# Linear attention with a gated projection: bonus products, one decay per unit, more load buffers, and another place for the output projection

## The chip, the cores and the metric

The kernel runs on one core of a Trainium2 chip. The metric is the device time of one execution in microseconds (us), the median of several executions. "Span" is the time from the first to the last instruction that the trace of an execution shows. The span is listed to 0.1 us.

The engines are TensorE (PE, with its weight loads as PEld), VectorE (DVE), ScalarE (ACT), GpSimd (POOL) and SyncE (SP, which issues the loads and stores).

## The reference

An attention of the RWKV kind: each head keeps a 48 x 48 state that decays by `w` at each step, and the newest token gets a bonus `u`. Its result goes into a gated linear unit whose gate is a causal convolution over five steps.

```python
# r, k, v: (4, 8, 768, 48); w, u: (8, 48); all float32
for t in range(S):
    cur = einsum('bhd,bhe->bhde', u * k[t], v[t])            # bonus of the newest token
    y[t] = einsum('bhd,bhde->bhe', r[t], state + cur)
    state = w * state + einsum('bhd,bhe->bhde', k[t], v[t])
x = y.transpose(0, 2, 1, 3).reshape(B, S, 384)
gate = sigmoid(causal depthwise conv of x, 5 taps)
out = (gate * (x @ w_val)) @ w_out
```

## The kernel before

A chunk is 128 steps, and two chunks are a unit. Each of the four sequences has three units, so there are twelve. The state passes from unit to unit within a sequence. The bonus of a token is its `v` scaled by one number per head, `dv`; TensorE adds it into the attention output as a product of `dv` with the identity.

The functions that the change touches:

```python
ld  = tile_pool(name="ld",  bufs=6)    # k and v as loaded
ldr = tile_pool(name="ldr", bufs=5)    # r as loaded

def state(n, cl):                      # KV: k^T v of one chunk
    kv_ps = ...                        # an own PSUM tile for each chunk
    for p in range(NP):
        matmul(out=kv_ps[:, p], lhsT=ks[:, cl, p], rhs=v of two heads, start=(p == 0), ...)

def carry(n, cl):                      # ID: adds the state that came in
    vector.tensor_tensor(out=kv_ps, in0=kv_ps, in1=zin, op=add)

def decay(n, cl):                      # ZE: state of the next chunk
    z = wk.tile(...)
    vector.tensor_tensor(out=z, in0=kv_ps, in1=wcm, op=mult)     # wcm = w**128

def y_out(n, cl):                      # Y: attention output, transposed
    # [cut: 12 narrow products of the state with r, 16 of scores with v]
    for G in range(3 * NP):            # the bonus: 12 products of 32 columns, last
        mm(G, dv[:, cl, 32 * G : 32 * G + 32], ident, last=True)

def project(n, cl):                    # O: three products 128 x 384
    o_ps = ps_at.tile(...)             # the PSUM pool (4 buffers) that the scores A use too
```

The order of work is written by hand. For units 4 to 11 it is this text, where `Y:-1.0` means chunk 0 of the unit before. Tokens of different engines run side by side; each engine takes its own in this order.

```
Y:-1.0 YE:-1.0 Y:-1.1 A:0.1 YE:-1.1 M:0.3 A:0.0 RS:1.0 M:0.2 KS:1.0 M:0.0 CV:0.0 C:-1.0
S:0.0 M:0.1 RT:1.0 V:-1.0 SE:0.0 SG:-1.0 HT:-1.0 V:-1.1 KV:0.0 SG:-1.1 RE:1.0 HT:-1.1
ID:0.0 KT:1.0 KE:1.0 O:-1.1 O:-1.0 OE:-1.1 ZE:0.0 PR:1.0 KV:0.1 ID:0.1 OE:-1.0 ZE:0.1
DV:0.0
```

Y attention output, A scores, C convolution, S bonus sums, RT and KT transposes, V value products, KV state products and O output projection run on TensorE. M (masks), SE (copy of the sums), HT (gated products), ID, ZE and PR run on VectorE. The copies YE, OE, RE and KE, the cast CV of v and the sigmoid SG run on ScalarE; RS, KS and DV on GpSimd.

Of the kernel before, what the change touches and what calls it, by code (L numbers as in the profile page):

```python
# [8 lines left out]
F32 = mybir.dt.float32  # L9
# [7 lines left out]
def kernel(  # L17
# [21 lines left out]
    U = 2  # L39
# [5 lines left out]
    persist = ctx.enter_context(tc.tile_pool(name="persist", bufs=1))  # L45
    ld = ctx.enter_context(tc.tile_pool(name="ld", bufs=6))
    ldr = ctx.enter_context(tc.tile_pool(name="ldr", bufs=5))
    wk = ctx.enter_context(tc.tile_pool(name="wk", bufs=2))
# [48 lines left out]
    for dst, src in ((wt, w), (ut, u)):  # L97
# [15 lines left out]
    nc.vector.tensor_copy(io_f, io_i32)  # L113
    sc_k = consts.tile([128, 1], F32)
    nc.vector.tensor_scalar(
        sc_k, io_f, scalar1=-1.0, scalar2=float(C - 1), op0=ALU.mult, op1=ALU.add
    )
    io_m = consts.tile([128, 2], mybir.dt.int32)
    nc.vector.tensor_single_scalar(io_m, io_j, C - 1, op=ALU.bitwise_and)
    sc_r = consts.tile([128, 2], F32)  # L120
    nc.vector.tensor_copy(sc_r, io_m)
    nc.vector.tensor_scalar_add(sc_r, sc_r, float(-C))
# [20 lines left out]
    nc.scalar.activation(out=lnw_bc, in_=w_bc, func=AF.Ln)  # L143
    dk = consts.tile([128, H, D], F32)
    dr = consts.tile([128, H, 2, D], F32)
    for j in range(2):
        nc.scalar.activation(
            out=dr[:, :, j, :], in_=lnw_bc, func=AF.Exp, scale=sc_r[:, j : j + 1]
        )
    nc.scalar.activation(out=dk, in_=lnw_bc, func=AF.Exp, scale=sc_k)  # L150

# [27 lines left out]
    wcm = consts.tile([128, NP, 2, D], F32)  # L179
    nc.gpsimd.memset(wcm, 0.0)  # L180


# [74 lines left out]
    def scale_k(n, eng, cls=(0, U)):  # L257
        cs = slice(*cls)
        eng.tensor_tensor(  # L259
            out=ks_t[n % 3][:, cs, :, :, 0:D].rearrange("p c n a d -> p c (n a) d"),  # L260
            in0=k_st[n][:, cs],
            in1=dk[:, None, :, :].to_broadcast([128, cls[1] - cls[0], H, D]),
            op=ALU.mult,
        )
# [42 lines left out]
    def bonus(n):  # L307
        if n == 0:
            kv_ps = ps_mm.tile([128, 512], F32, name="mm_ps")
        else:  # L310
            kv_ps = ps_kv.tile([128, 512], F32, name="kv_ps")
            st["kv_tile", n, 0] = kv_ps
        s_ps = kv_ps[:, DM : DM + U * H].rearrange("p (c h) -> p c h", c=U)
# [53 lines left out]
    def state(n, cl, idle=0):  # L367
        ks, vb = ks_t[n % 3], vb_t[n % 4]
        kv_ps = st.get(("kv_tile", n, cl))
        if kv_ps is None:  # L370
            kv_ps = ps_kv.tile([128, 512], F32, name="kv_ps")
        warm(kv_ps[:, 0:C], idle)
        kv_ps = kv_ps[:, 0:DM].rearrange("p (n a d) -> p n a d", n=NP, a=2)
        for p in range(NP):
            nc.tensor.matmul(  # L375
                out=kv_ps[:, p],
                lhsT=ks[:, cl, p].rearrange("p a x -> p (a x)"),
                rhs=heads(vb[:, cl], H)[:, 2 * p : 2 * p + 2, :],
                start=(p == 0),
                stop=(p == NP - 1),  # L380
                skip_group_check=True,
            )
        st["kv_ps", n, cl] = kv_ps
# [5 lines left out]
    def decay(n, cl):  # L389

        z = wk.tile([128, NP, 2, D], BF16, name="z", bufs=6)
        nc.vector.tensor_tensor(out=z, in0=st["kv_ps", n, cl], in1=wcm, op=ALU.mult)  # L392
        nn, cc = (n, 1) if cl == 0 else (n + 1, 0)
        st["zin", nn, cc] = z

    def y_out(n, cl, idle=0):
# [3 lines left out]
        warm(y_ps[:, 0], idle)  # L400
        first = set()

        def mm(G, lt, rh, last=False):
# [4 lines left out]
                rhs=rh,  # L408
                start=q not in first,
                stop=last,  # L410
                skip_group_check=True,
            )
            first.add(q)

# [6 lines left out]
        for x in range(2):  # L421
            for h in range(H):
# [4 lines left out]
                    vb[:, cl, 64 * h + c0 : 64 * h + c0 + 32],  # L427
                    at[:, par, p, :],
                )
        for G in range(3 * NP):  # L430
            mm(G, dv[:, cl, 32 * G : 32 * G + 32], ident, last=True)
        st["y_ps", n, cl] = y_ps
# [201 lines left out]
    def ok(n):  # L634
# [18 lines left out]
        S:3.0 SE:3.0 RT:4.0 M:3.1 A:3.1 KV:3.0 ZE:3.0 M:3.3 RE:4.0 C:2.0 KV:3.1 KS:4.0 V:2.1  # L653
        SG:2.1 V:2.0 M:3.2 HT:2.1 SG:2.0 ID:3.1 O:1.0 OE:1.0 KT:4.0 HT:2.0 O:1.1 PR:4.0 O:2.1
        KE:4.0 O:2.0 ZE:3.1 OE:2.1 DV:3.0 OE:2.0 OE:1.1
    """
    STEP = """
        Y:-1.0 YE:-1.0 Y:-1.1 A:0.1 YE:-1.1 M:0.3 A:0.0 RS:1.0 M:0.2 KS:1.0 M:0.0 CV:0.0 C:-1.0
        S:0.0 M:0.1 RT:1.0 V:-1.0 SE:0.0 SG:-1.0 HT:-1.0 V:-1.1 KV:0.0 SG:-1.1 RE:1.0 HT:-1.1
        ID:0.0 KT:1.0 KE:1.0 O:-1.1 O:-1.0 OE:-1.1 ZE:0.0 PR:1.0 KV:0.1 ID:0.1 OE:-1.0 ZE:0.1  # L660
        DV:0.0
    """
    TAIL = """
        Y:11.0 Y:11.1 YE:11.0 YE:11.1 CL:11.0 CL:11.1 VL:11.0 GL:11.0 VL:11.1 HL:11.0 GL:11.1
        HL:11.1 OL:11.0 XL:11.0 OL:11.1 XL:11.1
    """
    HEAD_STEPS = 4
    KBUFS, RBUFS = 6, 5
    loads = LOADS.split()
# [26 lines left out]
    nc.scalar.activation(out=wct, in_=wt, func=AF.Ln)  # L696
    nc.scalar.activation(out=wct, in_=wct, func=AF.Exp, scale=float(C))
    for par in range(2):
# [55 lines left out]
    def run(text, i):  # L754
        for tok in text.split():
# [5 lines left out]
            if name not in ("WV", "WP", "WO", "TL"):  # L761
                if not ok(n) or (name in ("KV", "ID", "ZE") and c == NU * U - 1):
                    continue
                if name == "ID" and c == 0:
                    continue
# [39 lines left out]
```

## Time and profile before

| | before |
|---|---|
| time, median of 3 | 107.12 us (106.53 to 108.38) |
| span of the profiled execution | 107.2 us |
| TensorE / VectorE busy | 93.5 / 76.9 us |
| first mask of unit 4, of unit 11 | 42.25 us, 93.30 us |

The first mask of a unit is the handiest mark in this trace. It starts when the scores of the unit are ready, and the distance from one to the next is the length of a unit. The seven distances were 7.37, 10.09, 6.40, 6.99, 6.67, 6.41 and 7.12 us. The second holds a stop of TensorE.

The lines that carry the argument are in the prediction.

### The profile page before, as it was taken

The numbers are of one execution on the slowest core, as the hardware profiler recorded it, in microseconds if no ns is written. First come the engines' busy times: TensorE is split into PE (matmuls) and PEld (weight loads), VectorE is DVE, ScalarE is ACT, GpSimd is POOL, SyncE is SP. The second block draws the span as 40 slices with busy tenths as digits, with TensorE's granted clock in tenths as the row PEclk, the third lists the DMA queues.
The fourth block names the chain that finished last, engine by engine and source line by source line (L and its number), as shares of the span: only waits on it lengthen the run. The fifth ranks groups of instructions, "written<-read, shape, count | busy, mean of one in ns | idle before, by whom it ended". The sixth has DMA issues, their size and how long they took to land.

```text
span 107.2 us, 5221 instructions
## 1 busy us (share of the span) xinstructions
PE 93.5 (87%) x2301; PEld 74.7 (70%) x2301; DVE 76.9 (72%) x153; ACT 73.2 (68%) x122; POOL 64.4 (60%) x64
## 2 busy tenths in 40 slices
PE   4996775999999999999299999999999989999770
PEld 4694664777887876868187878867889777876730
DVE  5395965484969793798428789899869798894050
ACT  4179625935997949896076889776898868845520
POOL 7957487566929976496089079495793965023000
PEclk9999999557999999999859999999999999999999
DMA  0999969989998969989696969798999992310404
GB/s 11 219 234 231 238 113 169 312 254 254 211 193 173 241 123 251 185 160 270 111 209 172 224 133 247 146 257 156 217 256 358 367 362 99 111 45 6 147 6 147
DMA packets 67491, 20.41 MB, mean 190 GB/s; under 512 B 63494, under 2 KB 67468, under 8 KB 67468
## 3 DMA queue, kind: packets, MB, share of 16 engines
q1 hardware_dynamic: 66492, 19.97, 81.3%
q8 instruction: 18, 0.29, 1.2%
q10 hardware_dynamic: 976, 0.10, 0.7%
q14 instruction: 5, 0.04, 0.1%
HBM read 15.35 MB, written 4.72 MB: 187 GB/s over the span
## 4 chain that ended last, share of the span: by engine, by line
PE 45%; SPq 15%; DVE 11%; issue 9%; DMA 9%; POOL 5%; ACT 3%; DVEq 0%; POOLq 0%
SPq L71 10%; DMA r_st<-in_r_dram 9%; PE mm_ps L405 9%; PE mm_ps L453 7%; PE at_ps L509 5%; PE at_ps L475 4%; PE at_ps L244 4%; PE at_ps L347 4%; POOL rs L230 3%; DVE at L360 3%; DVE hT L497 2%; PE at_ps L484 2%; PE kv_ps L375 2%; DVE z L392 2%; DVE kv_ps L387 2%
## 5 line engine op out<-in xcount | busy, mean ns | idle before, releaser
L360 DVE TENSOR_TENSOR at<-at_ps,mask 128x512 bf16<-128x512 f32 x48 | 30.4, 683 | 7.5 <-PE at_ps L347 7.4
L332 POOL TENSOR_TENSOR dv<-v_st,s_sb 128x768 bf16<-128x768 f32 x12 | 17.7, 1476 | 25.7 <-DVE s_sb L329 24.4
L259 POOL TENSOR_TENSOR ks<-k_st,dk 128x768 bf16<-128x768 f32 x11 | 20.4, 1858 | 2.6 <-DMA k_st<-in_k_dram 1.6
L230 POOL TENSOR_TENSOR rs<-r_st,dr 128x768 bf16<-128x768 f32 x10 | 18.2, 1820 | 2.4 <-DMA r_st<-in_r_dram 2.4
L252 ACT COPY rT<-at_ps 128x1024 bf16<-128x1024 bf16 (+1 forms) x13 | 15.8, 1229 | 4.0 <-PE at_ps L244 4.0
L453 PE MATMUL mm_ps<-xT,cwd 64*64 64x128 bf16 (+1 forms) x440 | 12.7, 255 | 3.3 <-issue 2.7
L466 ACT ACTIVATE gate<-mm_ps 128x384 bf16<-128x384 f32 x22 | 9.6, 487 | 8.5 <-PE mm_ps L453 8.5
L497 DVE TENSOR_TENSOR hT<-at_ps,gate 128x384 bf16<-128x384 f32 x22 | 11.7, 555 | 4.8 <-PE at_ps L484 4.7
L292 ACT COPY kT<-tr_ps 128x1024 bf16<-128x1024 bf16 x11 | 11.2, 1015 | 5.4 <-PE tr_ps L283 3.5
L453 PEld LDWEIGHTS <-cwd 64*64 64x64 bf16 x440 | 11.0, 111 | 4.8 <-issue 3.6
L437 ACT CAST xT<-mm_ps 128x384 bf16<-128x384 f32 x24 | 11.5, 485 | 3.9 <-PE mm_ps L405 3.3
L509 PE MATMUL at_ps<-wout,hT 128*128 128x384 bf16 x66 | 13.5, 327 | 0.2
L392 DVE TENSOR_TENSOR z<-kv_ps,wcm 128x384 bf16<-128x384 f32 x20 | 11.1, 555 | 0.9 <-PE kv_ps L375 0.5
L521 ACT COPY o_sb<-at_ps 128x384 f32<-128x384 f32 x22 | 9.7, 490 | 2.8 <-PE at_ps L509 2.8
L475 PE MATMUL at_ps<-xT,wval 128*128 128x256 bf16 x66 | 11.5, 286 | 0.0
L268 ACT CAST vb<-v_st 128x768 bf16<-128x768 f32 x12 | 10.1, 841 | 0.0
L347 PE MATMUL at_ps<-rT,kT 48*128 48x128 bf16 x192 | 8.8, 225 | 1.5 <-ACT kT L292 1.3
L405 PE MATMUL mm_ps<-at,vb 128*32 128x128 bf16 x384 | 9.8, 223 | 0.3 <-DVE at L360 0.3
L387 DVE TENSOR_TENSOR kv_ps<-kv_ps,z 128x384 f32<-128x384 f32 x16 | 8.9, 557 | 0.9 <-PE kv_ps L375 0.9
L300 DVE TENSOR_TENSOR pr<-tr_ps,rT 128x1024 bf16<-128x1024 bf16 x11 | 7.6, 688 | 1.7 <-ACT kT L292 1.2
L509 PEld LDWEIGHTS <-hT 128*128 128x128 bf16 x66 | 5.7, 98 | 4.5 <-DVE hT L497 2.2
L244 PE MATMUL at_ps<-ident,rs 128*128 128x128 bf16 x96 | 8.2, 234 | 0.1
(94 smaller groups left out, 151.2 us busy)
## 6 DMA issues: line engine op xcount, KB each, us to landing
r_st<-in_r_dram SPq DMA_DIRECT2D x12, 384.0 KB, 5.4
k_st<-in_k_dram SPq DMA_DIRECT2D x24, 192.0 KB, 4.8
v_st<-in_v_dram SPq DMA_DIRECT2D x24, 192.0 KB, 4.9
out_dram<-o_sb SPq DMA_DIRECT2D x11, 384.0 KB, 5.1
wv_st<-in_moe_w_val_dram SPq DMA_DIRECT2D x1, 576.0 KB, 5.5
wo_st<-in_moe_w_out_dram SPq DMA_DIRECT2D x1, 576.0 KB, 6.3
out_dram<-o_l SPq DMA_DIRECT2D x1, 192.0 KB, 1.9
out_dram<-o_l ACTq DMA_DIRECT2D x1, 96.0 KB
```

The lines of the kernel that those rows point to most:

```text
L230: eng.tensor_tensor(out=rs_t[n % 2][:, :, ps[0] : ps[1], :, 0:D].rearrange("p s n a d -> p (n a) s d"), in0=r_st[n][:, hs], in1=dr[:, hs], ...
L252: nc.scalar.copy(out=st["rT", n][:, ps[0] : ps[1], :].rearrange("x n (i s) -> x s n i", s=2), in_=st["r_tr", n, ps[0]],)
L259: eng.tensor_tensor(out=ks_t[n % 3][:, cs, :, :, 0:D].rearrange("p c n a d -> p c (n a) d"), in0=k_st[n][:, cs], in1=dk[:, None, :, :].to_ ...
L332: eng.tensor_tensor(out=dv_t[n % 2].rearrange("p c (h d) -> p (c h) d", d=D), in0=v_st[n].rearrange("p c h d -> p (c h) d"), in1=st["s", n ...
L347: nc.tensor.matmul(out=at_ps[par][:, p, :], lhsT=kT[rows, p, cs], rhs=rT[rows, p, cs], start=(p == 0), stop=(p == NP - 1), skip_group_chec ...
L360: nc.vector.tensor_tensor(out=st["at", n, cl][:, par], in0=st["at_ps", n, cl][par], in1=mask[:, None, :].to_broadcast([128, NP, 128]), op= ...
L392: nc.vector.tensor_tensor(out=z, in0=st["kv_ps", n, cl], in1=wcm, op=ALU.mult)
L405: nc.tensor.matmul(out=y_ps[32 * q : 32 * q + 32, T, :], lhsT=lt, rhs=rh, start=q not in first, stop=last, skip_group_check=True,)
L453: nc.tensor.matmul(out=g_ps[i][64 * qo : 64 * qo + 64, o0 : o0 + n0], lhsT=cwd[rows, T, t, :], rhs=xT[rows, T, t0 + c0 + t : t0 + c0 + t + ...
L475: nc.tensor.matmul(out=v_ps[:, 0:W], lhsT=wval[:, kt, i, :], rhs=xT[:, kt, t0 : t0 + W], start=(kt == 0), stop=(kt == NT - 1), skip_group_ ...
L497: nc.vector.tensor_tensor(out=st["hT", n][:, i], in0=st["v_ps", n, i], in1=st["gate", n][:, i], op=ALU.mult)
L509: nc.tensor.matmul(out=o_ps, lhsT=hT[:, i, c0 : c0 + C], rhs=wout[:, k, :], start=(j == 0), stop=(j == 2),)
```

## The change

The intent: less work on TensorE and VectorE, loads further ahead, and an output projection that fills the time in which the attention outputs are copied. It has four parts. The bonus becomes three full-width products at the head of Y. The second chunk adds onto the first in PSUM, so a unit needs one carry instead of two, and the decay factors are per unit. Loads get two more buffers each. O now belongs to two units back and stands between the Ys of the next step.

```diff
-    ld = ...(name="ld", bufs=6)
-    ldr = ...(name="ldr", bufs=5)
+    ld = ...(name="ld", bufs=8)
+    ldr = ...(name="ldr", bufs=7)
 # [cut: k is scaled by factors for each chunk, r for the unit; bdm, a mask of ones; wcm = w**256]
 def state(n, cl):
-        kv_ps = st.get(("kv_tile", n, cl))
-        if kv_ps is None:
-            kv_ps = ps_kv.tile([128, 512], F32, name="kv_ps")
+        kv_ps = st["kv_tile", n]             # [cut: opened once in a unit]
-                start=(p == 0),
+                start=(p == 0 and cl == 0),
 def decay(n, cl):
-        nc.vector.tensor_tensor(out=z, in0=st["kv_ps", n, cl], in1=wcm, op=ALU.mult)
+        nc.vector.tensor_tensor(
+            out=z, in0=st["kv_ps", n, cl], in1=bdm if cl == 0 else wcm, op=ALU.mult
+        )
 def y_out(n, cl):
+        for T in range(NT):                      # first: 3 products of 128 columns
+            nc.tensor.matmul(out=y_ps[:, T, :], lhsT=dv[:, cl, T * 128 : T * 128 + 128],
+                             rhs=ident, start=(T == 0), stop=False, ...)
-        for G in range(3 * NP):
-            mm(G, dv[:, cl, 32 * G : 32 * G + 32], ident, last=True)
 # the order of units 4 to 11 (head and tail follow it)
-        Y:-1.0 YE:-1.0 Y:-1.1 A:0.1 ... HT:-1.1 ID:0.0 KT:1.0 KE:1.0 O:-1.1 O:-1.0 OE:-1.1
-        ZE:0.0 PR:1.0 KV:0.1 ID:0.1 OE:-1.0 ZE:0.1 DV:0.0
+        Y:-1.0 O:-2.0 YE:-1.0 OE:-2.0 Y:-1.1 O:-2.1 A:0.1 YE:-1.1 OE:-2.1 ... HT:-1.1 ID:0.0
+        KT:1.0 KE:1.0 ZE:0.0 PR:1.0 KV:0.1 ZE:0.1 DV:0.0
-    KBUFS, RBUFS = 6, 5
+    KBUFS, RBUFS = 8, 7
```

More of the change, by code (lines that the diff above doesn't have):

```diff
@@ L45 @@
     persist = ctx.enter_context(tc.tile_pool(name="persist", bufs=1))
-    ld = ctx.enter_context(tc.tile_pool(name="ld", bufs=6))
-    ldr = ctx.enter_context(tc.tile_pool(name="ldr", bufs=5))
+    ld = ctx.enter_context(tc.tile_pool(name="ld", bufs=8))
+    ldr = ctx.enter_context(tc.tile_pool(name="ldr", bufs=7))
     wk = ctx.enter_context(tc.tile_pool(name="wk", bufs=2))
@@ L113 @@
     nc.vector.tensor_copy(io_f, io_i32)
-    sc_k = consts.tile([128, 1], F32)
-    nc.vector.tensor_scalar(
-        sc_k, io_f, scalar1=-1.0, scalar2=float(C - 1), op0=ALU.mult, op1=ALU.add
-    )
-    io_m = consts.tile([128, 2], mybir.dt.int32)
-    nc.vector.tensor_single_scalar(io_m, io_j, C - 1, op=ALU.bitwise_and)
+    sc_k = consts.tile([128, U], F32)
+    for cl in range(U):
+        nc.vector.tensor_scalar(
+            sc_k[:, cl : cl + 1], io_f, scalar1=-1.0, scalar2=float(C - 1 - cl * C),
+            op0=ALU.mult, op1=ALU.add,
+        )
     sc_r = consts.tile([128, 2], F32)
-    nc.vector.tensor_copy(sc_r, io_m)
+    nc.vector.tensor_copy(sc_r, io_j)
     nc.vector.tensor_scalar_add(sc_r, sc_r, float(-C))
@@ L143 @@
     nc.scalar.activation(out=lnw_bc, in_=w_bc, func=AF.Ln)
-    dk = consts.tile([128, H, D], F32)
+    dk = consts.tile([128, U, H, D], F32)
     dr = consts.tile([128, H, 2, D], F32)
@@ L149 @@
         )
-    nc.scalar.activation(out=dk, in_=lnw_bc, func=AF.Exp, scale=sc_k)
+    for cl in range(U):
+        nc.scalar.activation(
+            out=dk[:, cl], in_=lnw_bc, func=AF.Exp, scale=sc_k[:, cl : cl + 1]
+        )
     def ring(name, shape, n, dtype=BF16):
@@ L180 @@
     nc.gpsimd.memset(wcm, 0.0)
+    bdm = consts.tile([128, NP, 2, D], F32)
+    nc.gpsimd.memset(bdm, 0.0)
+    for par in range(2):
+        nc.gpsimd.memset(bdm[64 * par : 64 * par + 64, :, par, :], 1.0)
     wv_st = consts.tile([128, NT, DM], F32)
@@ L261, in scale_k @@
             in0=k_st[n][:, cs],
-            in1=dk[:, None, :, :].to_broadcast([128, cls[1] - cls[0], H, D]),
+            in1=dk[:, cs],
             op=ALU.mult,
@@ L311, in bonus @@
             kv_ps = ps_kv.tile([128, 512], F32, name="kv_ps")
-            st["kv_tile", n, 0] = kv_ps
+            st["kv_tile", n] = kv_ps
         s_ps = kv_ps[:, DM : DM + U * H].rearrange("p (c h) -> p c h", c=U)
@@ L368, in state @@
         ks, vb = ks_t[n % 3], vb_t[n % 4]
-        kv_ps = st.get(("kv_tile", n, cl))
-        if kv_ps is None:
-            kv_ps = ps_kv.tile([128, 512], F32, name="kv_ps")
-        warm(kv_ps[:, 0:C], idle)
+        if ("kv_tile", n) not in st:
+            st["kv_tile", n] = ps_kv.tile([128, 512], F32, name="kv_ps")
+        kv_ps = st["kv_tile", n]
+        if cl == 0:
+            warm(kv_ps[:, 0:C], idle)
         kv_ps = kv_ps[:, 0:DM].rearrange("p (n a d) -> p n a d", n=NP, a=2)
@@ L391, in decay @@
         z = wk.tile([128, NP, 2, D], BF16, name="z", bufs=6)
-        nc.vector.tensor_tensor(out=z, in0=st["kv_ps", n, cl], in1=wcm, op=ALU.mult)
+        nc.vector.tensor_tensor(
+            out=z, in0=st["kv_ps", n, cl], in1=bdm if cl == 0 else wcm, op=ALU.mult
+        )
         nn, cc = (n, 1) if cl == 0 else (n + 1, 0)
@@ L400, in y_out @@
         warm(y_ps[:, 0], idle)
-        first = set()
+        for T in range(NT):
+            nc.tensor.matmul(
+                out=y_ps[:, T, :],
+                lhsT=dv[:, cl, T * 128 : T * 128 + 128],
+                rhs=ident,
+                start=(T == 0),
+                stop=False,
+                skip_group_check=True,
+            )
         def mm(G, lt, rh, last=False):
@@ L408, in mm @@
                 rhs=rh,
-                start=q not in first,
+                start=False,
                 stop=last,
@@ L412, in mm @@
             )
-            first.add(q)
         z = st.get(("zin", n, cl))
@@ L428, in y_out @@
                     at[:, par, p, :],
+                    last=True,
                 )
-        for G in range(3 * NP):
-            mm(G, dv[:, cl, 32 * G : 32 * G + 32], ident, last=True)
         st["y_ps", n, cl] = y_ps
@@ L653 @@
         S:3.0 SE:3.0 RT:4.0 M:3.1 A:3.1 KV:3.0 ZE:3.0 M:3.3 RE:4.0 C:2.0 KV:3.1 KS:4.0 V:2.1
-        SG:2.1 V:2.0 M:3.2 HT:2.1 SG:2.0 ID:3.1 O:1.0 OE:1.0 KT:4.0 HT:2.0 O:1.1 PR:4.0 O:2.1
-        KE:4.0 O:2.0 ZE:3.1 OE:2.1 DV:3.0 OE:2.0 OE:1.1
+        SG:2.1 V:2.0 M:3.2 HT:2.1 SG:2.0 O:1.0 OE:1.0 KT:4.0 HT:2.0 O:1.1 PR:4.0
+        KE:4.0 ZE:3.1 DV:3.0 OE:1.1
     """
     STEP = """
-        Y:-1.0 YE:-1.0 Y:-1.1 A:0.1 YE:-1.1 M:0.3 A:0.0 RS:1.0 M:0.2 KS:1.0 M:0.0 CV:0.0 C:-1.0
-        S:0.0 M:0.1 RT:1.0 V:-1.0 SE:0.0 SG:-1.0 HT:-1.0 V:-1.1 KV:0.0 SG:-1.1 RE:1.0 HT:-1.1
-        ID:0.0 KT:1.0 KE:1.0 O:-1.1 O:-1.0 OE:-1.1 ZE:0.0 PR:1.0 KV:0.1 ID:0.1 OE:-1.0 ZE:0.1
-        DV:0.0
+        Y:-1.0 O:-2.0 YE:-1.0 OE:-2.0 Y:-1.1 O:-2.1 A:0.1 YE:-1.1 OE:-2.1 M:0.3 A:0.0 RS:1.0
+        M:0.2 KS:1.0 M:0.0 CV:0.0 C:-1.0 S:0.0 M:0.1 RT:1.0 V:-1.0 SE:0.0 SG:-1.0 HT:-1.0 V:-1.1
+        KV:0.0 SG:-1.1 RE:1.0 HT:-1.1 ID:0.0 KT:1.0 KE:1.0 ZE:0.0 PR:1.0 KV:0.1 ZE:0.1 DV:0.0
     """
     TAIL = """
-        Y:11.0 Y:11.1 YE:11.0 YE:11.1 CL:11.0 CL:11.1 VL:11.0 GL:11.0 VL:11.1 HL:11.0 GL:11.1
+        Y:11.0 Y:11.1 YE:11.0 YE:11.1 O:10.0 O:10.1 OE:10.0 OE:10.1 CL:11.0 CL:11.1 VL:11.0 GL:11.0 VL:11.1 HL:11.0 GL:11.1
         HL:11.1 OL:11.0 XL:11.0 OL:11.1 XL:11.1
@@ L696 @@
     nc.scalar.activation(out=wct, in_=wt, func=AF.Ln)
-    nc.scalar.activation(out=wct, in_=wct, func=AF.Exp, scale=float(C))
+    nc.scalar.activation(out=wct, in_=wct, func=AF.Exp, scale=float(W))
     for par in range(2):
@@ L763, in run @@
                     continue
-                if name == "ID" and c == 0:
+                if name == "ID" and (c == 0 or j):
                     continue
```

## The prediction

> **What bounds the kernel now.** I read the page first, then the chain of waits in order of time, then the timelines of VectorE and of the DMA-issuing queue. Four parts of the page:
>
> ```profile
> PE 93.5 (87%) x2301; PEld 74.7 (70%) x2301; DVE 76.9 (72%) x153; ACT 73.2 (68%) x122; POOL 64.4 (60%) x64
> ...
> PEclk9999999557999999999859999999999999999999
> DMA  0999969989998969989696969798999992310404
> ...
> q8 instruction: 18, 0.29, 1.2%
> ```
>
> TensorE (PE) is the busiest engine, DMA is nearly full until about 85 us, and the granted clock dips twice. 0.29 MB in 18 packets is 16 KB per instruction fetch; the program has 4601 PE rows, so one fetch is about 256 rows.
>
> The chain (start, length in us, what). First unit 5, then the unit from 58 us and the end of the next:
>
> ```profile
> 49.84 1.02 PE mm_ps L453 x38
> 50.85 2.22 issue
> 53.07 0.31 PE mm_ps L453 x2
> ...
> 58.10 1.23 PE mm_ps L405 x80
> 59.34 0.55 PE at_ps L347 x16
> ...
> 63.30 1.09 PE at_ps L509 x6
> 64.39 0.17 PE kv_ps L375 x4
> ...
> 70.54 0.57 DVE z L392
> 71.11 0.05 issue
> 71.15 0.34 PE kv_ps L375 x4
> 71.49 1.23 PE mm_ps L405 x80
> ```
>
> L405 is the attention output (Y), L347 the scores (A), L453 the convolution (C), L509 the output projection (O), L375 the state product (KV), L392 the decay (ZE). From 58.10 to 64.39 PE never waits: 6.29 us per unit, PE bound. In the next unit the second KV waits for the decay, and the unit takes 71.49 - 64.56 = 6.9 us. At 50.85 PE stands 2.22 us although nothing it waits for is late: an instruction fetch, shown below.
>
> VectorE in the same unit:
>
> ```profile
> 59.71 2.49 DVE L360 TENSOR_TENSOR at<-at_ps,mask 128x512 bf16<-128x512 f32 x4 [0.87 <-PE at_ps L347]
> 62.11 0.17 DVE L329 COPY s_sb<-kv_ps 128x16 f32<-128x16 f32 x1
> 62.30 1.05 DVE L497 TENSOR_TENSOR hT<-at_ps,gate 128x384 bf16<-128x384 f32 x2
> 63.27 0.55 DVE L392 TENSOR_TENSOR z<-kv_ps,wcm 128x384 bf16<-128x384 f32 x1
> ```
>
> From the first mask to the end of the first decay are 4.11 us, all but filled. That decay ends at 63.82; O on PE runs to 64.39, so the projection hides it with 0.57 us to spare. This slot is what the change empties.
>
> [...] Counting PE rows, the gaps at 50.85 (2.22 us), 68.86 (0.23), 73.72 (0.20), 87.24 (0.33) and 100.58 (0.61) stand at rows 1977, 2745, 3001, 3769, 4281: distances of 256 or multiples. [...] The worst was rows 1721 to 1976, Y, A and C alone, in 2.75 us.
> [...] after the 2.22 us the work from the bonus sums to the state product took 2.92 us against 1.65 in the next unit, 1.27 lost.
> [...] 80 products of Y in 1.23 us are 15.4 ns each, while eight full transposes take 0.45 to 0.47, 57 ns each.
> [...] So the second KV must still wait for the decay's read. At 71.15 it starts 0.05 us after the decay ends.
>
> **The change part by part.**
> Bonus products: 12 narrow ones (12 x 15.4 = 0.185 us) become 3 full ones (3 x 57 = 0.17 us) in each of 24 outputs: about 0.4 us at most. What counts is 216 fewer products, 432 fewer rows (4169). They now stand first in Y, so Y needs dv at its start.
> Decay once: the second chunk adds onto the first in PSUM, and 8 of 16 carries (L387, 0.56 us, spaced 0.59) go: 4.7 us of VectorE. But the removed carry stands behind the first decay, off the path carry, decay, second KV. Where the first decay is at the end of the path the gain is near zero.
> Setup: three more memsets on GpSimd and one more 0.6 us exponential on ScalarE. They fall into idle times of 1.07 us (waiting for u) and 0.67 us (waiting for the first transposes): nothing.
> Load buffers: the issuing queue is without a real gap until its last load:
>
> ```profile
> 70.19 3.33 SPq L71 DMA_DIRECT2D v_st<-in_v_dram  x2
> 74.02 0.37 SPq L78 DMA_DIRECT2D r_st<-in_r_dram  x1
> 74.50 2.77 SPq L71 DMA_DIRECT2D v_st<-in_v_dram  x2
> 77.33 21.43 SPq L525 DMA_DIRECT2D out_dram<-o_sb  x11
> ```
>
> The last r (74.02) reuses the buffer of r6, scaled at 46.33: free 26 us before. Loads go as fast as DMA takes them; more buffers give nothing.
> The fetch: a unit falls from 372 to 336 rows, and two projections (12 rows in 1.09 us) thin out the dense part. [...] I expect the stalls gone: 2.22 + 1.27 at unit 5, about 0.4, 0.2 and 0.4 at three others, 0.6 in the tail; about 5 us.
> The moved projection. The new PE order is KV, Y, O, Y, O, A, A, C, S, RT, V, V, KV, KT, and again KV. I follow one unit from the start of the second KV (0), with lengths from the trace: KV and its start 0.34, Y 0.60, O 0.545, A 0.275 each, C 1.02, S 0.285, RT 0.47, V 0.50 each. Y and O twice: first A at 2.63, its first mask at 3.01 (0.38 later at 71.49 + 1.23 = 72.72, mask 73.10). The second A needs the PSUM buffer of the second O: that ends at 2.63, its copy takes 0.45 on ScalarE, so the second A starts near 3.2 instead of 2.9. C ends at 4.5, S 4.8, RT 5.26, V 5.76 and 6.26. VectorE: masks 3.01 to 5.4, sums 5.4, gated products at 5.86 and 6.36 (each 0.1 after its V), then, where no carry comes, decay 6.86 to 7.42; second KV at 7.47. With the carry (0.59 before): 8.03. PE itself was free at 6.88, so it waits 0.6 and 1.15 us. In the last unit of a sequence there is no second KV; there Y waits for dv (sums 5.42, then 0.24, then 1.48 on GpSimd: 7.2), and the first mask comes 6.9 after the last one.
> Three units: 7.47 + 8.03 + 6.9 = 22.4 us, where before 59.71 to 79.77 took 20.06 with 0.6 of fetch stalls. From the first mask of unit 4 (42.25 before, about the same after) to that of unit 11: unit 4 takes 9.0 (its second A waits for three copies in a row on ScalarE), then 6.9, 7.47, 8.03, 6.9, 7.47, 8.03, together 53.8. Before: 93.30 - 42.25 = 51.05. That is +2.75, the fetch gain already in it.
> Tail: after the last mask start, Y needs dv (4.2), Y twice 1.2, O 1.09, so the last convolution starts at 6.5 instead of 99.09 - 93.30 = 5.8: +0.7, less the 0.6 of the stall.
> Head: one carry before a bonus sum goes (a PE wait of 0.27): -0.3.
> Sum: 107.2 + 2.75 + 0.1 - 0.3 = 109.75.
>
> **The rivals.**
> First: the fetch was the real limit and the rest has more slack than I count. Then the 5 us come out whole and the time is 102.5 to 104. For it: the stall is in plain sight and the change looks made against it. Against: 0.57 us of slack behind the decay can't take 1.09 us of moved projection.
> Second: the second A doesn't hold up VectorE, since its copy comes sooner. Each of seven units is then up to 0.33 shorter: 107.4, the gains and losses cancelling.
> Third: VectorE loses 4.7 us and was the bound in the carry units, so they fall to the PE time of 6.3: about 105. Against: the removed carry isn't on the path to the second KV.
> Fourth: the new waits of about 1 us drop the clock as the 2.22 us did: 112 or more. Against: the 1.2 us wait at 70 us cost no clock.
> Fifth: deeper buffers fill DMA earlier and slow the instruction fetch; little, as the queue is full already.
>
> **Range and chances.** The chain gives 109.75; the second rival pulls down by 2.3, the first by more, the fourth up. I put the time at 109.0 us and 105.3 to 111.8 for 8 in 10. Within 2% is 105.0 to 109.3, so the estimate is near its upper edge: slower 0.45, same 0.40, faster 0.15.
>
> **What would show it.** No PE gap of over 1 us at a 256-row boundary, and no clock dip past 30 us. Waits of PE before the second KV for the decay in two of three units, 0.6 and 1.1 us. The second A waiting for a copy on ScalarE, near 0.3 us. VectorE about 72 us busy with idle time before the masks of near 1 us. Units of 7.5, 8.0 and 6.9 us between first masks. The load queue ending near 77 us still. I am wrong if PE runs through the second KV without waiting, if a fetch stall of 2 us remains, or if loads end several us sooner.

107.2 + 2.75 + 0.1 - 0.3 = 109.75 us is complete, lowered to 109.0 for the rivals. That the stalls would go was the author's estimate; why TensorE stops at some of the boundaries and not at others is not shown. That the second KV waits for the decay in the changed kernel too was assumed; its trace shows it (0.57 and 1.17 us).

A "block" is 256 rows of TensorE (products plus weight loads), an estimate from the page of before: 4601 rows for 18 packets of the instruction queue. The stops listed above lie whole multiples of 256 rows apart; I call these, and the like in other runs, fetch stops. That they are instruction fetches is inferred from this and from the shifted run below.

## The result, and the profile after

| | before | after |
|---|---|---|
| time, median of 4 | 106.83 us (105.42 to 108.38) | 113.75 us (113.24 to 114.85) |
| ratio of the fast runs | | 1.074 [1.061, 1.086] |
| span of the profiled execution | 107.2 us | 111.4 us (time 113.24) |
| TensorE / VectorE busy | 93.5 / 76.9 us | 95.3 / 72.6 us |
| first mask of unit 4, of unit 11 | 42.25, 93.30 us | 42.26, 97.00 us |

A ratio here is the mean time of one kernel's fast runs over that of the other's fast runs of the same rounds, so it isn't quite the ratio of the medians. The bracket is its 95% interval.

The change is slower by 7%; 109.0 us and at most 111.8 us were predicted. The page of the kernel after:

```profile
PE 95.3 (86%) x2085; PEld 72.8 (65%) x2085; DVE 72.6 (65%) x145; ACT 75.1 (67%) x123; POOL 65.5 (59%) x67
...
PEclk9999599759999999999999999999999999999997
...
q8 instruction: 16, 0.26, 1.1%
```

VectorE has lost 4.3 us of work and the instruction queue two packets, as was meant. The granted clock was 1.00 from 30 to 108.6 us, to the end of the last product; before had a dip to 0.50 from 53 to 56 us. TensorE, with 216 fewer products, is busy for longer, not shorter.

Now one unit of TensorE after the change. The columns are start, length, engine, line, operation, operands, count and, in brackets, the idle time before with its releaser. L383 is KV, L290 the transposes KT, L412 the bonus, L423 the rest of Y, L525 O, L354 A:

```profile
68.92 0.61 PE L290 MATMUL tr_ps<-ident,ks 128*128 128x128 bf16 x8
70.70 0.33 PE L383 MATMUL kv_ps<-vb,ks 128*128 128x96 bf16 x4 [1.17 <-DVE z L400]
70.87 0.33 PE L412 MATMUL mm_ps<-ident,dv 128*128 128x128 bf16 x3
71.13 0.35 PE L423 MATMUL mm_ps<-rT,z 128*32 128x128 bf16 x12
...
71.64 0.66 PE L525 MATMUL at_ps<-wout,hT 128*128 128x384 bf16 x3
72.13 0.33 PE L412 MATMUL mm_ps<-ident,dv 128*128 128x128 bf16 x3
...
72.90 0.66 PE L525 MATMUL at_ps<-wout,hT 128*128 128x384 bf16 x3
73.50 0.45 PE L354 MATMUL at_ps<-rT,kT 48*128 48x128 bf16 x9
74.13 0.38 PE L354 MATMUL at_ps<-rT,kT 48*128 48x128 bf16 x7 [0.18 <-ACT o_sb L537]
```

Between KT and the second KV, where O stood, TensorE now waits 1.17 us for the decay. Read distances between starts, not the modelled lengths: from 70.70 to the first scores at 73.50 are 2.80 us. The second half of the scores waits 0.18 us for a copy of O on ScalarE.

What VectorE did meanwhile. L367 is the mask, L513 the gated products, L395 the carry, L400 the decay:

```profile
65.64 2.49 DVE L367 TENSOR_TENSOR at<-at_ps,mask 128x512 bf16<-128x512 f32 x4 [1.34 <-PE at_ps L354]
...
68.53 1.05 DVE L513 TENSOR_TENSOR hT<-at_ps,gate 128x384 bf16<-128x384 f32 x2 [0.32 <-PE at_ps L500]
69.50 0.56 DVE L395 TENSOR_TENSOR kv_ps<-kv_ps,z 128x384 f32<-128x384 f32 x1
70.09 0.56 DVE L400 TENSOR_TENSOR z<-kv_ps,bdm 128x384 bf16<-128x384 f32 x1
...
73.94 0.69 DVE L367 TENSOR_TENSOR at<-at_ps,mask 128x512 bf16<-128x512 f32 x1 [2.11 <-PE at_ps L354]
```

The two engines take turns. From the first mask at 65.64 to the second KV at 70.70 are 5.06 us; they end with a chain on VectorE: gated products, carry and decay. Before it VectorE idles 0.32 us, because the gated products wait for the value products V on TensorE, so a late second half of the scores delays this stretch too (4.78 us in a run below, where they don't wait). From there to the next first mask at 73.94 are 3.24 us, set by TensorE, and VectorE idles 2.11 us of them. Their sum, 8.30 us, is the length of the unit. A unit without a carry takes 58.12 to 62.58 to 65.64: 4.46 plus 3.06, so 7.52.

Before, in the unit whose first mask is at 59.71, the second KV started at 64.23 and the next first mask at 66.11: 4.52 plus 1.88. So the stretch up to the second KV was as long as it is now, with the projection inside it, beside VectorE's chain: the decay ended at 63.82, and TensorE was still at O. Now the projection stands in the second stretch, in series with that chain.

### The profile page after: what moved, and what is told of

Its sections match the earlier page's. It is cut to its first block, busy times and chain, and to the rows that moved or that the text cites. A ratio compares the mean times of both kernels' runs of the same rounds, so it can differ in the third digit from the quotient of the medians.

```text
span 111.4 us, 4777 instructions
## 1 busy us (share of the span) xinstructions
PE 95.3 (86%) x2085; PEld 72.8 (65%) x2085; DVE 72.6 (65%) x145; ACT 75.1 (67%) x123; POOL 65.5 (59%) x67
## 4 chain that ended last, share of the span: by engine, by line
PE 21%; issue 21%; POOL 19%; DMA 16%; ACT 8%; SPq 6%; DVE 3%; POOLq 2%; DVEq 0%
POOL ks L266 10%; POOL rs L237 8%; DMA v_st<-in_v_dram 8%; DMA k_st<-in_k_dram 5%; SPq L71 4%; DMA r_st<-in_r_dram 3%; PE mm_ps L469 3%; PE mm_ps L423 3%; ACT kT L299 3%; PE at_ps L525 2%; PE at_ps L354 2%; SPq L78 2%; POOL dv L339 2%; PE mm_ps L412 2%; PE tr_ps L290 1%
## 5 line engine op out<-in xcount | busy, mean ns | idle before, releaser
L367 DVE TENSOR_TENSOR at<-at_ps,mask 128x512 bf16<-128x512 f32 x48 | 30.3, 684 | 16.9 <-PE at_ps L354 16.8
L525 PE MATMUL at_ps<-wout,hT 128*128 128x384 bf16 x66 | 14.2, 329 | 0.0
L513 DVE TENSOR_TENSOR hT<-at_ps,gate 128x384 bf16<-128x384 f32 x22 | 11.6, 556 | 3.6 <-PE at_ps L500 3.5
L354 PE MATMUL at_ps<-rT,kT 48*128 48x128 bf16 x192 | 10.1, 219 | 3.2 <-ACT o_sb L537 1.8
L469 PE MATMUL mm_ps<-xT,cwd 64*64 64x128 bf16 (+1 forms) x440 | 12.0, 255 | 0.0
L537 ACT COPY o_sb<-at_ps 128x384 f32<-128x384 f32 x22 | 10.6, 483 | 1.9 <-PE at_ps L525 0.9
L383 PE MATMUL kv_ps<-vb,ks 128*128 128x96 bf16 x80 | 7.2, 217 | 4.8 <-DVE z L400 4.6
L354 PEld LDWEIGHTS <-kT 48*128 48x128 bf16 x192 | 5.8, 94 | 8.2 <-issue 5.8
L469 PEld LDWEIGHTS <-cwd 64*64 64x64 bf16 x440 | 10.0, 111 | 1.2
L491 PE MATMUL at_ps<-xT,wval 128*128 128x256 bf16 x66 | 10.8, 273 | 0.0
L412 PE MATMUL mm_ps<-ident,dv 128*128 128x128 bf16 x72 | 8.2, 224 | 2.0 <-POOL dv L339 1.8
L423 PE MATMUL mm_ps<-at,vb 128*32 128x128 bf16 x384 | 9.6, 219 | 0.0
L383 PEld LDWEIGHTS <-ks 128*128 128x128 bf16 x80 | 5.3, 103 | 5.9 <-issue 5.6
```

The source lines that it names most:

```text
L354: nc.tensor.matmul(out=at_ps[par][:, p, :], lhsT=kT[rows, p, cs], rhs=rT[rows, p, cs], start=(p == 0), stop=(p == NP - 1), skip_group_chec ...
L367: nc.vector.tensor_tensor(out=st["at", n, cl][:, par], in0=st["at_ps", n, cl][par], in1=mask[:, None, :].to_broadcast([128, NP, 128]), op= ...
L383: nc.tensor.matmul(out=kv_ps[:, p], lhsT=ks[:, cl, p].rearrange("p a x -> p (a x)"), rhs=heads(vb[:, cl], H)[:, 2 * p : 2 * p + 2, :], sta ...
L423: nc.tensor.matmul(out=y_ps[32 * q : 32 * q + 32, T, :], lhsT=lt, rhs=rh, start=False, stop=last, skip_group_check=True,)
L469: nc.tensor.matmul(out=g_ps[i][64 * qo : 64 * qo + 64, o0 : o0 + n0], lhsT=cwd[rows, T, t, :], rhs=xT[rows, T, t0 + c0 + t : t0 + c0 + t + ...
L525: nc.tensor.matmul(out=o_ps, lhsT=hT[:, i, c0 : c0 + C], rhs=wout[:, k, :], start=(j == 0), stop=(j == 2),)
```

## The experiments

There are sixteen runs, in four sets; each set ran on one chip with its own runs of the kernel before. "Time" is the median; every run was correct.

| run | time, us | ratio to before [95%] |
|---|---|---|
| O moved, nothing else | 111.71 | 1.067 [1.053, 1.080] |
| all but the move of O | 105.43 | 1.010 [1.000, 1.020] |
| after, both O ahead of the second Y | 112.03 | 1.069 [1.059, 1.080] |
| bonus alone | 104.51 | 0.994 [0.983, 1.006] |
| decay alone | 106.93 | 1.016 [1.004, 1.028] |
| buffers alone | 108.73 | 1.026 [0.988, 1.064] |
| after, with narrow bonus products last | 113.11 | 1.078 [1.055, 1.102] |
| before, shifted by 112 rows | 104.94 | 0.992 [0.980, 1.003] |
| decay alone, shifted by 112 rows | 107.23 | 1.013 [1.003, 1.024] |
| pair: decay, paired bonus, O in its old place | 103.90 | 0.980 [0.969, 0.991] |
| after again | 113.95 | 1.072 [1.060, 1.084] |
| after with ten useless products | 113.82 | 1.070 [1.057, 1.083] |

The theory: the moved projection comes into series with VectorE's chain and costs nearly all of the loss. The rivals: the cost lies in the other parts (bonus, decay, buffers); or TensorE is short of throughput or of instructions; or the kernel before was profiled in an unusual execution, so that part of the loss lies in the base.

### The parts of the change

**Before, again.** No edit: the scatter and the stop in unit 5.

> The kernel before, unchanged, profiled once more. Theory 1 (the profile used for the prediction caught a slow execution): the measured time of the changed kernel is 1.84 us above the span of its profile, so an ordinary execution of before (106.8 us) should have a span near 105.0; then the 2.22 us fetch gap and the dip of the clock at 50 us are missing or under 1 us here, and masks of unit 4 to unit 11 take about 48 us instead of 51. Theory 2 (the fetch gap is in every execution): a gap of about 2 us at the same row, span 107, time above the span by nothing.

Four runs gave 104.96 to 109.02 us, with spans of 103.1 to 107.1. The profile fell on the slowest, with a stop of 1.92 us at the same instruction in unit 5. So before scatters by 4%, and its profile had once more shown the slow end.

**O moved, nothing else.**

```diff
-  Y:-1.0 YE:-1.0 Y:-1.1 A:0.1 YE:-1.1 ... KT:1.0 KE:1.0 O:-1.1 O:-1.0 OE:-1.1 ZE:0.0 ... OE:-1.0
+  Y:-1.0 O:-2.0 YE:-1.0 OE:-2.0 Y:-1.1 O:-2.1 A:0.1 YE:-1.1 OE:-2.1 ... KT:1.0 KE:1.0 ZE:0.0 ...
```

> Before, with the output projection moved between the next step's attention outputs and nothing else. Theory 1 (the moved projection empties the slot before the second state product): 1.05 to 1.08 of before, TensorE waiting 0.6 to 1.2 us before that product in two of three units, units of about 7.5, 8.2 and 6.7 us. Theory 3 (the parts at the other places cost it: bonus products first, accumulation in one tile): 0.98 to 1.02.

The order of the head and the tail was changed to match. The ratio is 1.067, nearly the whole loss. One fetch stop of 0.88 us is left, in unit 5. The waits of TensorE ahead of the second KV (now L375), without and with a carry, are those of the full change:

```profile
62.20 0.33 PE L375 MATMUL kv_ps<-vb,ks 128*128 128x96 bf16 x4 [0.57 <-DVE z L392]
...
70.32 0.34 PE L375 MATMUL kv_ps<-vb,ks 128*128 128x96 bf16 x4 [1.17 <-DVE z L392]
```

It has the old two carries per unit, and the wait doesn't differ by a hundredth. The carry that the change removes is not on the path, as predicted.

**All but the move of O.** The changed kernel with the old order of tokens.

```diff
 # after, with
+  ... ID:0.0 KT:1.0 KE:1.0 O:-1.1 O:-1.0 OE:-1.1 ZE:0.0 PR:1.0 KV:0.1 ID:0.1 OE:-1.0 ZE:0.1 DV:0.0
 # [cut: head and tail to match; the changed kernel skips ID:0.1]
```

> The changed kernel with the projection at its place in before. Theory 1: 0.97 to 1.00 of before, units of 6.4 to 6.7 us, no wait over 0.3 us before the second state product. Theory 3: near the changed kernel, 1.05 or more.

The ratio is 1.010, and no fetch stop of TensorE is left. Three parts together bring nothing even so; I had expected 0.97 to 1.00. A unit without a carry takes 6.54 us, where before took 6.40, and the first mask of unit 4 comes at 42.73 us. For the units the trace says why. KV, then the two Ys of a unit, here and in the kernel before:

```profile
61.14 0.33 PE L383 MATMUL kv_ps<-vb,ks 128*128 128x96 bf16 x4
61.31 0.33 PE L412 MATMUL mm_ps<-ident,dv 128*128 128x128 bf16 x3
61.57 0.41 PE L423 MATMUL mm_ps<-at,vb 128*32 128x128 bf16 x16
61.91 0.34 PE L412 MATMUL mm_ps<-ident,dv 128*128 128x128 bf16 x3
...
62.69 0.62 PE L354 MATMUL at_ps<-rT,kT 48*128 48x128 bf16 x16
```

```profile
64.23 0.33 PE L375 MATMUL kv_ps<-vb,ks 128*128 128x96 bf16 x4
64.49 0.41 PE L405 MATMUL mm_ps<-at,vb 128*32 128x128 bf16 x16
64.73 0.34 PE L405 MATMUL mm_ps<-ident,dv 128*32 128x128 bf16 x12
...
65.56 0.62 PE L347 MATMUL at_ps<-rT,kT 48*128 48x128 bf16 x16
```

Sixteen narrow products take 0.24 us when narrow ones follow (64.49 to 64.73) and 0.34 us when full-width ones follow (61.57 to 61.91). KV takes 0.17 us when full-width products follow (61.14 to 61.31) and 0.26 us when narrow ones do (64.23 to 64.49). Each passage between a full-width and a narrow group costs about 0.1 us, in either direction. From KV to the scores it is 1.55 us against 1.33. (That these are costs of switching the width is read from the spacing; no run isolates it.)

**After, with both O ahead of the second Y.**

```diff
-  Y:-1.0 O:-2.0 YE:-1.0 OE:-2.0 Y:-1.1 O:-2.1 A:0.1 YE:-1.1 OE:-2.1 ...
+  Y:-1.0 O:-2.0 O:-2.1 YE:-1.0 OE:-2.0 Y:-1.1 OE:-2.1 A:0.1 YE:-1.1 ...
```

> The changed kernel with both projections ahead of the second attention output, so that the copy of the second one is done before the second score product needs its buffer. If the wait of the second scores for that copy holds up the unit (as predicted: 0.3 us in each of seven units), this takes off 0.2 to 0.35 us from the units with a second state product, 1.5 to 2 us in all: 1.055 of before. If it doesn't matter: 1.07 as the changed kernel.

The copies of O come sooner, the second half of the scores no longer waits for them, one passage between widths is saved (from the second KV to the scores it is 2.69 us instead of 2.80, in units with a carry), and the seven units together shrink from 54.74 to 52.41 us. The waits for the decay stay at 1.17 and 0.57 us. In the times this gain isn't clear of noise: the ratio of 1.069 isn't told apart from 1.074 and 1.072 for the change in its own sets, and it is not the 1.055 that I had expected if the wait mattered. So the units show that the wait for a copy and the passage were worth something, and most of the loss is elsewhere.

**Bonus alone.**

```diff
-        for G in range(3 * NP):
-            mm(G, dv[:, cl, 32 * G : 32 * G + 32], ident, last=True)
+        for T in range(NT): ...   # 3 full-width products, first
```

> Before with the bonus products alone changed (three of full width first, in place of twelve narrow ones last). Theory A (prediction: 0.17 us in place of 0.185, a gain of up to 0.4 us in all): 0.99 to 1.00 of before's fast runs. Theory B (read off the first runs: in the kernel with everything but the moved projection the two attention outputs of a unit take 1.38 us where before they take 1.07, so switching between full and narrow products costs 0.15 us per output): on a TensorE-bound loop 12 units x 0.31 us = 3.7 us at most, less where TensorE has slack or a fetch gap goes: 1.01 to 1.04.

The ratio is 0.994, not told apart from one. No fetch stop shows, and all four runs lie within 1%, where before scatters by 5% in this set. Unit 5 takes 6.53 us, where before takes 7.38 in its fastest profile; a unit without a carry takes 6.54 instead of 6.40, and from KV to the scores it is 1.55 us as above. So the missing stop gives what the passages take back. Whether the stop went because there are fewer instructions or because they fall into other blocks is not told apart: a run below loses it with more instructions.

**Decay alone.**

```diff
-                start=(p == 0),
+                start=(p == 0 and cl == 0),
-            in1=wcm
+            in1=bdm if cl == 0 else wcm      # with wcm = w**256, factors per chunk, no second carry
```

> Before with the decay once per unit alone. Theory: the removed carry lies behind the decay that the second state product waits for, so little: 0.985 to 1.0 of before; VectorE 4.5 us less busy. If the accumulation in one tile brings a new wait: 1.02 or more.

This missed my expectation of 0.985 to 1.0: the ratio is 1.016, although VectorE is 4 us less busy (72.6). Its profile shows TensorE stopped for instructions for 1.56 us in unit 5 and for 1.16 us in the tail; more on it below.

**Buffers alone.**

```diff
-    KBUFS, RBUFS = 6, 5
+    KBUFS, RBUFS = 8, 7        # and the pools to match
```

> Before with the eight and seven load buffers alone. Theory: the load queue is limited by the transfers, not by free buffers, so 0.995 to 1.01, and the last load issued at 74 to 77 us as before. Rival: loads run ahead, the last one 4 us sooner, and the fetch gaps grow.

The ratio of 1.026 has an interval that holds one. The loads don't come sooner: the queue turned to the stores at 77.88 us, against 77.33 before. The profile is of a slow execution with three fetch stops of over 1 us, so it says nothing on whether deeper buffers disturb the fetch. The whole change and the run with all but the move of O have the deeper buffers and no fetch stop, but other instruction counts too.

**After, with narrow bonus products last**, as before.

```diff
 # after, with
+        for G in range(3 * NP):
+            mm(G, dv[:, cl, 32 * G : 32 * G + 32], ident, last=True)
```

> The changed kernel with the narrow bonus products last, as before. If the full products cost 0.15 us per output on the path from the second state product to the masks, and the early need of dv holds up the last unit of a sequence and the tail: 0.3 us off each of seven units, 0.6 more off two of them and 0.7 off the tail, 3 to 4 us in all, 1.03 to 1.045 of before. If they cost nothing: 1.065 to 1.075 as the changed kernel.

This was a miss of mine. I expected the time to fall to 1.03 to 1.045 of before, because the passages between widths and the early need of `dv` would go. The ratio is 1.078, from two fast runs. The passages did not go: units of 7.52 and 8.29 us are those of the full change, 7.52 and 8.30. With O between the outputs a full-width group stands between narrow ones anyhow, so the passages are as many. Only the last unit of a sequence gets shorter, 6.79 and 6.84 us instead of 7.25. There the bonus comes first in the changed kernel and waits for `dv`.

### Is TensorE waiting, or short?

**After again, and after with ten useless products** in the emptied slot. They go into the PSUM tile that the next Y opens anyway, from unit 4 on.

```diff
 def state(n, cl):
+        elif n >= 4:                       # only ahead of the second chunk
+            st["y_open", n] = ps_mm.tile([128, NT, 128], F32, name="mm_ps")
+            warm(st["y_open", n][:, 0], 10)      # ten 128 x 128 products of the identity
```

> The whole change once more, as the base of the filler run on the same chip. Both theories: 1.06 to 1.085 of before, waits of TensorE ahead of the second state product 1.17 us in units with a carry and 0.57 us in units without, no gap in instruction fetch.

> The change plus ten useless full products (about 0.57 us by the rate of other 128x128 products) between the key transposes and the second state product, from unit 4 on. Theory that the emptied slot is pure waiting on the decay chain of VectorE: the time stays that of the change within 0.5 per cent, and the listed waits ahead of the second state product shrink from 1.17 to about 0.6 and from 0.57 to about 0. Rival, TensorE's own work or its instruction supply bounds the changed kernel: the time grows by 0.57 us in each unit that has them, about 2.7 to 2.9 us or 2.5 per cent.

Times are 113.95 and 113.82 us. In their profiles the first masks of units 4 to 11 agree within 0.03 us. The run with the useless products (L132):

```profile
62.16 0.72 PE L132 MATMUL mm_ps<-ident 128*128 128x128 bf16 x10
62.88 0.33 PE L386 MATMUL kv_ps<-vb,ks 128*128 128x96 bf16 x4
...
69.67 0.72 PE L132 MATMUL mm_ps<-ident 128*128 128x128 bf16 x10
71.00 0.33 PE L386 MATMUL kv_ps<-vb,ks 128*128 128x96 bf16 x4 [0.61 <-DVE z L403]
```

The first wait is gone and the second is 0.61 us instead of 1.17, at no cost. TensorE was only waiting there.

### The base: which execution of before was it?

**Looks at before.** No edit.

> One more profile of the kernel before, hoped to be of a fast execution (span near 103). If the fetch gap is what parts the fast executions from the slow ones: no TensorE gap over 1 us at 50 us, and unit 4's first mask to unit 11's in 47 to 49 us. If it falls in the slow state again, it shows the gap of about 2 us a third time and tells nothing new.

> One more look at before, for a profile of a fast execution. Theory: an execution with a span near 103 us lacks the gap of about 2 us in unit 5 and has units of 6.3 to 6.6 us; a slow one near 107 us has it. Rival: the gap is in both, and the two groups differ elsewhere.

> As the look before it: a span near 103 us should come without the gap in unit 5, one near 107 us with it.

The first look had a span of 106.3 us and a stop of 2.16 us. The other two had spans of 103.5 and 105.3 us; the stop in each:

```profile
50.66 0.24 PE L453 MATMUL mm_ps<-xT,cwd 64*64 64x128 bf16 x2 [0.86 <-issue]
```

```profile
51.41 0.24 PE L453 MATMUL mm_ps<-xT,cwd 64*64 64x128 bf16 x2 [1.96 <-issue]
```

My expectation missed in one point: the fast execution does not lack the stop; it has a shorter one, 0.86 us. All five stand ahead of the same instruction, after 38 of 40 products of the convolution. With the stop goes the length of unit 5: 7.38 us with 0.86, 8.48 with 1.96, and 10.09 with 2.22. In the first pair the 1.10 us of difference is the stop alone, without a clock dip in unit 5 (granted clock 1.00 from 45 to 58 us in both). In the last the clock dip comes on top: the granted clock is 0.50 from 53 to 56 us. The length of the stop doesn't decide on the dip: it follows the stop of 1.92 us in the second profile of before (0.5 in the slice from 53.6 to 56.2 us), and not that of 1.96.

This settles what the base was. A fast execution of before needs 48.12 us for the seven units, the one in the prediction 51.05. (It is a single run, 105.40 us, a little below the fastest of the eight others in its set, 105.55.)

**Before, shifted by 112 rows:** 56 tiny products in the head move every later instruction of TensorE against the blocks of 256 rows (the estimate beside the prediction).

```diff
 def attn(n, cl):
+        if n == 1 and cl == 1:
+            for _ in range(56):
+                matmul(out=at_ps[0][:, 0, 0:8], lhsT=ident, rhs=ident[:, 0:8], ...)
```

> Before with 56 tiny products (112 rows) put on TensorE where it waits near 19 us, so that the 256-row fetch blocks fall elsewhere in the later program. If the gaps are fetches: the gap of 2 us in unit 5 goes, the gap in the tail goes, and smaller ones (up to 1 us each) stand after the blocks that now hold the least work (rows 1465, 2233, 3257, 4025 on, 3.0 to 3.5 us of work each by the lengths of the trace); fewer executions in the slow state, 104 to 106 us. If the gaps have another cause: a gap of 2 us stays in unit 5.

Ratio 0.992 with useless work added, and all four runs at 104.2 to 105.9. The stop in unit 5 is gone, and so is the one in the tail. Two others came, at two of the four boundaries that I had named, both inside value products:

```profile
58.47 0.49 PE L481 MATMUL at_ps<-xT,wval 128*128 128x256 bf16 x3 [0.78 <-DVE s_sb L329]
...
91.43 0.27 PE L481 MATMUL at_ps<-xT,wval 128*128 128x256 bf16 x1 [0.74 <-issue]
```

In rows of TensorE (products plus weight loads) these are 2489 and 4281. The old stop was at 1977; the distances are 2 x 256 and 9 x 256. The stops stay on the boundaries of blocks while the program moves under them. The name in the first bracket, `s_sb`, is the latest semaphore (its copy ended at 58.27, 0.20 us before); by its row I take the stop for one of the fetch. The seven units take 46.88 us. Unit 6, with the stop of 0.78, takes 7.34; other units of its kind take 6.40. So my estimate for before without any stop is 46.88 - 0.94 = 45.94 us, and all stops in the loop of the fast look cost 48.12 - 45.94 = 2.2 us.

**Decay alone, shifted likewise.**

> Decay once per unit alone, with the same 112 rows of shift. If the decay alone was at 1.016 because of fetch gaps (1.56 us in unit 5, 1.16 in the tail of its profile): 0.98 to 1.0 of before's fast runs. If the accumulation itself costs: still 1.01 or more.

Ratio 1.013: the shift does not cure it. One stop of 1.33 us stands at the same row as the 0.78 of the run above. Its seven units take 47.58 us against 46.88 there, and its head ends 1.7 us later. Why the head is later stays open.

### A version that keeps what was good

**Pair.** Decay once per unit, O in its old place, six and five buffers, and the full-width bonus products of both outputs together ahead of all narrow ones (from unit 3 on), so that they cost one passage and not three. Eighteen tiny products in the head (36 rows) shift the fetch blocks; how many it takes was the author's estimate.

```diff
 def y_out(n, cl):
+        for c in (0, 1) if pair and cl == 0 else ...:
+            st["y_open", n, c] = y_ps = ps_mm.tile(...)
+            for T in range(NT):
+                matmul(out=y_ps[:, T, :], lhsT=dv[:, c, T * 128 : T * 128 + 128], rhs=ident, ...)
```

> An attempt to beat both: decay once, projection where before has it, full-width bonus products of both outputs of a unit together ahead of the narrow ones (one switch of width in place of two), and 36 rows of shift[...]. If switches cost 0.15 us and fetch gaps are gone: units of 6.4 to 6.6 us, no gap over 0.5 us, 0.97 to 0.99 of before's fast runs. If TensorE stays the bound with the full products at 0.09 us each: 0.99 to 1.0.

Six runs gave 103.9 us, ratio 0.980 [0.969, 0.991]: it beats both kernels. In its trace the pair of Ys has one passage inside it, no fetch stop is left, a unit with a carry takes 6.73 us and one without 6.32. The seven units take 46.04 us, against 48.12 in a fast execution of before. But the 6.99 us of before for a unit with a carry hold a stop of 0.23 us; without one it takes 6.59 (the shifted run), and the estimate for the whole loop without stops was 45.94. So in the loop the gain is that the stops are gone; the pairing only keeps the full-width products from costing more (from KV to the scores it is 1.33 us, as before), and the decay once per unit shows no gain. Which of the three edits took the stops away was not taken apart.

## Why the prediction was wrong

Its mechanism held and its size did not. Two terms of its sum failed: the start, where a span of 107.2 us was taken for a time (1.85 us too low), and the cost of the moved projection, where "Y 0.60" measured 0.77. Point by point:

- **Waits for the decay ahead of the second KV: right.** 0.6 and 1.1 us announced (1.15 in its working), 0.57 and 1.17 measured, and the moved projection alone brings them. The filler run shows that they are pure waiting.
- **The second A waits for a copy: right**, 0.18 us instead of near 0.3. VectorE's idle time before the masks was larger than the near 1 us announced: 1.34 to 2.16.
- **Removed carries, more buffers: right, nothing gained.** The waits of the run that moved O alone equal those of the whole change; the load queue ended at 78.85 us.
- **No fetch stop and no clock dip left: right.** What it was worth was wrong, see below. One reading beside it doesn't hold: the "1.2 us wait at 70 us" isn't in the trace of before: TensorE waits there for about 0.2 us (O ends near 70.9, KV starts at 71.15). The clock dip didn't come with every long stop: the clock fell to 0.50 after stops of 2.22 and 1.92 us, and stayed at 1.00 after 1.96.
- **The projection's cost: mis-sized.** The step was "Y and O twice: first A at 2.63, its first mask at 3.01". Measured are 2.80 and 3.24 where both Ys have a state product. The term in it that failed is "Y 0.60": with 31 products it takes 0.77 us (70.87 to 71.64): 0.26 for the three full-width ones and 0.51 for 28 narrow ones. At the 57 and 15.4 ns of the prediction these are 0.17 and 0.43. The 0.17 left over is two passages between widths. Two Ys are 0.34 us too short. KV, taken as 0.34 for 0.17, gave 0.17 of it back; the mask came 0.06 later after the scores. The 7.47 for a unit without a carry came close by luck: there only the second Y is 0.17 too short, and the KV that is 0.17 too long cancels it (2.63 predicted, 62.58 to 65.21 measured). The carry of 0.59 on top of 7.47 is 8.06, not the 8.03 written.

Against the three kinds of unit and the seven in the loop:

| unit | predicted, us | measured, us | number |
|---|---|---|---|
| unit 4 | 9.0 | 8.61 | 1 |
| last of a sequence | 6.9 | 7.25 | 2 |
| without a carry | 7.47 | 7.52 | 2 |
| with a carry | 8.03 | 8.30, 8.29 | 2 |
| sum | 53.8 | 54.74 | 7 |

So the loop was 0.94 us short. The last unit of a sequence missed by most. Its wait for `dv` was foreseen (Y at 4.19 us after the first mask, measured 73.94 to 78.11, 4.17); the miss is the two Ys again, 0.35 us. The run with narrow products last made it 6.79 and 6.84 us, so some 0.4 us of it come from the bonus standing at the head of Y. The wait for `dv` in the tail is of the same kind; with narrow products last it is 0.68 us:

```profile
101.18 0.34 PE L412 MATMUL mm_ps<-ident,dv 128*128 128x128 bf16 x3 [1.18 <-POOL dv L339]
```

The other terms of the miss are not in the schedule. The sum of 4.75 us between 109.0 and 113.75 is made up like this:

| term | us |
|---|---|
| the span of 107.2 used where a time belongs | 1.85 |
| the chain, 109.75 for a span of 111.4: head 0.31, loop 0.94, tail 0.40 | 1.65 |
| 109.75 lowered to 109.0 for the rivals that pull down | 0.75 |
| the profiled run (113.24) is faster than the median | 0.51 |

The largest is the first. The sum began with 107.2, which is a span, and was then read as a time. The kernel before had no time listed for its profiled execution, and its median of 107.12 looked like a match. With the difference that all later runs show, 1.7 to 1.9 us, that execution took some 109 us (an estimate; the second profile of before has a span of 107.1 and a time of 109.02) and was slower than the median.

A second error hides in the ratio and not in this sum. "About 5 us" of fetch stalls were credited as a gain, from a slow execution of before. In the fast one the stop in unit 5 is 0.86 us and the clock does not dip there. So the change could gain far less than that against a fast run: 2.2 us in the loop by the estimate above. Span against span, fast against fast, the change loses 111.4 - 103.5 = 7.9 us: 54.74 - 48.12 = 6.62 in the seven units, 42.26 - 41.20 = 1.06 in the head and 0.22 in the tail. The head is not part of the shown cause: the first mask of unit 4 came anywhere from 40.67 to 43.71 us in the profiles, and from 40.85 to 42.25 in the five of before alone.

Of the rivals, the first ("the fetch was the real limit") fell with the filler and the fast look. The second ("the second A doesn't hold up VectorE") didn't come true by itself: the wait was there, and only another order of O took it away, for 2.3 us of the loop in one profile. The third ("VectorE was the bound in the carry units") fell with units of 8.30 us. The fifth, deeper buffers that slow the fetch, stays untested. The fourth, a clock drop through the new waits, did not come: with waits of 1.17 us the granted clock stayed at 1.00.

What stays open: why executions of before differ in the length of the same stop, why decay alone is slower than before, and what sets the length of the head.

## What to carry to other kernels

When work is moved from one slot to another, ask what the slot was hiding: here 1.09 us of projection lay beside a chain of another engine that was just as long, so taking it out freed nothing, and putting it in elsewhere cost its whole length. Price products in the order in which they run: here sixteen narrow ones took 0.24 us ahead of narrow ones and 0.34 ahead of full-width ones, about 0.1 us for the change of width, so group them by width. Before a prediction starts from a profile, check that the profiled execution is a typical one, and that span and time are not mixed up.
